# The two pairs of a couple in different PSUM tiles, in the first product by seven block products

## The chip, the core and the metric

The program runs on one core of a Trainium2 chip. The metric is the device time of one execution in microseconds (us); the time before is 593.28 us, the median of three runs (590.06, 593.28 and 599.59 us). One further execution was profiled; the profile shows for each engine when its instructions ran and what ended its idle time: TensorE (PE, with PEld for its weight loads), VectorE (DVE), ScalarE (ACT), GpSimd (POOL), and SyncE (SP), whose queue issues the transfers.

## What is computed

Attention with a narrow window and block summaries, followed by a feed-forward layer with the activation relu(h)². Cut to what matters here:

```python
x = attention(q, k, v)              # (3072, 512)
h = x @ w_in                        # w_in (512, 2048): the first product
g = np.maximum(h, 0.0) ** 2
return g @ w_out                    # w_out (2048, 512): the second product
```

All of it is float32. For TensorE each operand is split into a high and a low float32r part, and a product is the sum of three: high by high, low by high, high by low.

## The kernel before

The 3072 tokens are six units of 512. The first two units go through the feed-forward layer plainly. The other four go in two sets of two units (`s` = 0 and 1). In both sets the second product `g @ w_out` is made by seven block products (a Strassen-like scheme on 2 by 2 blocks, `products`), and in set 1 the first product `x @ w_in` is, too: that is `mixed`, the function that the change touches. It begins when the second product of set 0 ends, and the second product of set 1 follows it to the end of the program.

In `mixed` the 2048 rows of the hidden layer are eight **pairs** `p` = 0 to 7, each of two blocks of 128 rows; the model dimension has two halves, and the 1024 tokens of set 1 are two units. For every pair seven **steps** `j` = 0 to 6 are made, each one block product of six matmuls of 128x512 (`product`, L1647). I write (k, j) for step j of a couple's first pair (k = 0) or second pair (k = 1). Two pairs 2i and 2i+1 make a **couple**, and their steps are interleaved by a table: `COUPLE` is (0,2), (1,2), (0,3), (0,4), (1,3), (1,4), (0,6), (0,5), (1,6), (1,5). The first couple's table `FIRST_COUPLE` also holds steps 0 and 1 of pairs 0 to 3; steps 0 and 1 of pairs 4 to 7 (`BEGINS`) come before everything.

Steps 0, 2, 4 and 6 of a pair add up in one PSUM accumulator `x`, which is read between them: after step 0 (`Q1`), after step 2 (`Q2`), after step 4 (`Q3`) and after step 6 (`Q21`, or `R21` with the relu). So step 4 of a pair has to wait until its own `Q2` has read, and step 6 until its own `Q3` has. Steps 3 and 5 add up in another buffer (`sz`), step 1 in `att`. Pairs 0 to 3 are read by ACT (`evacuate`, L1661, and the relu L1740). Pairs 4 to 7, whose flag `apart` is set, are read by DVE with an addition (`plus`, L1666, which also reads `sz` and `att`); their step 0 lies in another buffer, so `x` begins with step 2. DVE further makes squares (L1674) and differences (L1682), ACT squares by relu and square (L1677, L1678).

The accumulators lie in two PSUM tiles, `o0` and `o1`, each of two halves of 128x512 float32 (2 KB per partition and half): `o_tiles[i // 2][:, i % 2]` for `i` = `slot`, 0 to 3. `Pair.slot` says which half a pair has; pairs p and p+4 have the same one. The same two tiles, whole, are the accumulators of `products` before and after (L1454): its first product in set 1 opens `o0`, its ninth `o1`. `old` names the last readers of the tiles from set 0, `mixed_end` the last readers in `mixed`.

The order of the instructions on every engine is made by a planner (`Plan`): tasks have due times and costs, and a list schedule with buffer counts gives the order, in which they are then emitted. In the planner the four halves are four separate buffers. The semaphore waits between engines are not written in the kernel: the layer below sets them from the tiles that each emitted instruction reads and writes.

Of the kernel before, what the change touches and what calls it, by code (L numbers as in the profile page):

```python
# [240 lines left out]
def attention_then_relu2_ffn(  # L241
# [1340 lines left out]
    def mixed():  # L1582
# [105 lines left out]
        class Pair:  # L1688
            def __init__(self, p):
                self.p, self.apart = p, p >= NQ // 2  # L1690
                self.g = Buf(kinds[f"w{NQ + p}"], (P, 4 * DM), F32, f"g{s}_{p}")
                self.parts = g_parts[s, p] = [Part(self.g, k * DM, (k + 1) * DM) for k in range(4)]
                self.slot = p // 2 % 2 * 2 + p % 2
                self.x = self.bank()

            def bank(self):
# [108 lines left out]
    for u in range(PLAIN + 2):  # L1805
# [14 lines left out]
        if u > PLAIN:  # L1820
            at, rest = unit_at[u], [(j, p) for j in range(SOON, PRODUCTS) for p in range(NQ)]
            rest.insert(NQ + 2, rest.pop(NQ - 1))
            for f in range(NF):
# [5 lines left out]
                for _ in range(WITH_ITEM[f]):  # L1829
                    j, p = rest.pop(0)  # L1830
# [81 lines left out]
```

## Time and profile before

| | |
|---|---|
| median of three runs | 593.28 us (590.06 to 599.59) |
| the profiled execution | 595.69 us, of which its span 592.7 us |
| PE busy | 575.2 us, 97% of the span |
| DVE busy | 443.3 us, 75% |
| ACT busy | 352.9 us, 60% |
| `mixed` after its steps 0 and 1 of pairs 4 to 7 | from 440.8 to 511.7 us |
| second product of set 1 | from 511.7 to 588.3 us |

The profile's views that are used: its page; the busy time of each engine in chosen stretches (engine, busy us, and in brackets the number of instructions; then the granted TensorE clock, the DMA engines' share and GB/s); the waits (who waited for whom: us in total, times, the longest); the chain of work that ended last; and the timeline (start us, duration us, engine, line, operation, what it writes and reads; in square brackets how long the engine was idle before it and what ended that). Buffer numbers are left out in the profile's names, so `o` is `o0` or `o1`, and `g` is a buffer of any pair.

### The profile page before, as it was taken

The page shows a single profiled execution, that of the slowest core. Times are in us where ns is not written, and L with a number is a line of the kernel's source. Part 1 is how long each engine was busy: PE and PEld are TensorE (multiplying, and loading weights), DVE is VectorE, ACT ScalarE, POOL GpSimd, SP SyncE. Part 2 cuts the span into 40 slices and gives each one's busy share as a digit, 9 for nine tenths or more (in the row PEclk, how much of TensorE's full clock was granted, in tenths as well). Part 3 has the DMA queues.
Part 4 walks back from the last instruction along what each step waited for, and adds up shares of the span by engine and source line. Part 5 has one row for each costly group of instructions (what it writes and reads, how often), then busy time and mean ns, then how long its engine had stood idle before and what let it go on. Part 6 is the DMA issues. An engine that isn't in the chain of part 4 may idle for free.

```text
span 592.7 us, 12046 instructions
## 1 busy us (share of the span) xinstructions
PE 575.2 (97%) x4084; PEld 467.6 (79%) x4084; DVE 443.3 (75%) x1018; ACT 352.9 (60%) x876; POOL 98.5 (17%) x165
## 2 busy tenths in 40 slices
PE   8999999999999999999999999999989999999997
PEld 6777878787788888888788888878778877788885
DVE  5899898777547729656976877999839865678764
ACT  1999876767636546645666567586546324654442
POOL 4300005153766014400300050000000000000000
PEclk9999999999999999999999999999989999999999
DMA  8999985869997878995989756898884445667772
GB/s 306 311 391 320 320 295 183 290 225 334 346 336 222 266 277 247 323 305 179 339 243 298 265 181 217 270 295 272 267 264 144 128 146 172 177 191 233 196 225 96
DMA packets 120272, 149.61 MB, mean 252 GB/s; under 512 B 10556, under 2 KB 79164, under 8 KB 120212
## 3 DMA queue, kind: packets, MB, share of 16 engines
q1 hardware_dynamic: 120212, 148.86, 77.1%
q8 instruction: 32, 0.52, 0.3%
q14 instruction: 28, 0.23, 0.1%
HBM read 103.99 MB, written 44.04 MB: 250 GB/s over the span
## 4 chain that ended last, share of the span: by engine, by line
PE 67%; DMA 11%; DVE 10%; ACT 4%; SPq 4%; issue 2%; POOL 2%; DVEq 0%; ACTq 0%
PE o L1454 23%; PE h L1340 14%; PE o L1074 8%; PE o L1647 7%; PE h L1050 6%; DMA raw<-wW 5%; PE sz L1647 3%; PE x L854 3%; DMA kb<-kT 2%; PE att L647 2%; PE att L1647 2%; SPq L841 1%; DMA a<-turn 1%; DVE g L1666 1%; DVE t L995 1%
## 5 line engine op out<-in xcount | busy, mean ns | idle before, releaser
L1454 PE MATMUL o<-gh,w 128*128 128x512 f32 x448 | 121.2, 392 | 0.0
L1436 ACT CAST gh<-g 128x512 fp32r<-128x512 f32 x112 | 68.6, 621 | 56.3 <-PE o L1454 26.5
L1454 PEld LDWEIGHTS o<-gh,w 128*128 128x128 f32 x448 | 83.3, 188 | 17.9 <-ACT gh L1436 0.3
L1441 DVE TENSOR_TENSOR gl<-g,gh 128x512 fp32r<-128x512 f32 x112 | 76.2, 692 | 21.7 <-ACT gh L1436 21.1
L1050 PE MATMUL h<-xh,w 128*128 128x512 f32 x240 | 74.8, 392 | 1.0 <-DVE w L1003 0.7
L1454 PE MATMUL o<-gl,w 128*128 128x512 f32 x224 | 69.5, 391 | 0.4 <-DVE gl L1441 0.3
L1340 PE MATMUL h<-xh,w 128*128 128x512 f32 x224 | 69.0, 389 | 0.0
L1074 PE MATMUL o<-w,gh 128*128 128x512 f32 x240 | 62.2, 395 | 0.4 <-DVE w L1003 0.2
L778 ACT ACTIVATE p<-p,small 128x118 f32<-128x118 f32 x160 | 61.1, 386 | 1.1 <-DVE small L721 0.8
L1050 PEld LDWEIGHTS h<-xh,w 128*128 128x128 f32 x240 | 44.8, 188 | 11.7 <-DVE w L1003 1.3
L1074 PEld LDWEIGHTS o<-w,gh 128*128 128x128 f32 x240 | 44.3, 188 | 10.8 <-ACT gh L1061 0.9
L1454 PEld LDWEIGHTS o<-gl,w 128*128 128x128 f32 x224 | 41.9, 188 | 10.0 <-DVE gl L1441 1.2
L1340 PEld LDWEIGHTS h<-xh,w 128*128 128x128 f32 x224 | 42.1, 188 | 8.7
L1050 PE MATMUL h<-xl,w 128*128 128x512 f32 x120 | 46.7, 389 | 0.0
L1340 PE MATMUL h<-xl,w 128*128 128x512 f32 x112 | 43.6, 389 | 0.0
L1350 ACT ACTIVATE r<-h 128x512 f32<-128x512 f32 x32 | 19.1, 597 | 37.7 <-PE h L1340 37.5
L660 POOL COPY kb<-kb 128x96 f32<-128x96 f32 x25 | 8.5, 339 | 194.7 <-PE att L647 107.3
L1064 DVE TENSOR_TENSOR gl<-r,gh 128x512 fp32r<-128x512 f32 x30 | 23.1, 771 | 19.4 <-ACT gh L1061 16.7
L721 DVE CUSTOM_DVE_ANT_0 p<-att,mask 128x118 f32<-128x118 f32 x152 | 33.1, 275 | 2.6 <-PE att L647 2.5
L1074 PE MATMUL o<-w,gl 128*128 128x512 f32 x120 | 33.6, 390 | 0.0
L1431 DVE TENSOR_TENSOR g<-g 128x512 f32<-128x512 f32 x48 | 32.8, 689 | 0.4
L778 ACT ACTIVATION_READ_ACCUMULATOR p<-p,small 128x1 f32 x160 | 30.5, 190 | 0.0
(209 smaller groups left out, 1079.6 us busy)
## 6 DMA issues: line engine op xcount, KB each, us to landing
raw<-wW SPq DMA_DIRECT2D x32, 512.0 KB
w<-scr_s SPq DMA_DIRECT2D x64, 256.0 KB
w<-scr_a SPq DMA_DIRECT2D x48, 256.0 KB
turn<-a SPq DMA_DIRECT2D x40, 256.0 KB
a<-turn SPq DMA_DIRECT2D x160, 64.0 KB
scr_t<-ci SPq DMA_DIRECT2D x32, 256.0 KB
w<-scr_i SPq DMA_DIRECT2D x32, 256.0 KB
w<-scr_t SPq DMA_DIRECT2D x32, 256.0 KB
```

The costliest lines, as they stand in the source:

```text
L721: nc.vector.tensor_tensor_reduce(out=pr.tile[:, j, :KEYS], in0=score_at(g, 0, j), in1=mask_of(g)[0], scale=-SCALE, scalar=-NEG, op0=ALU.ad ...
L778: nc.scalar.activation(x, score_tile(g, p % parts)[:, p] if by_pe else x, AF.Exp, bias=nm.tile[:, p : p + 1], scale=SCALE if by_pe else -1 ...
L1050: nc.tensor.matmul(cut(h), lhsT=lhs.tile[:, k * P : (k + 1) * P], rhs=rhs[:, k, c0 : c0 + n], start=(i == 0), stop=(i == 3 * KT - 1),)
L1064: lambda: nc.vector.tensor_tensor(out=cut(gl), in0=cut(r), in1=cut(gh).bitcast(F32), op=ALU.subtract),
L1074: nc.tensor.matmul(o_of(o, t), lhsT=terms[i][0].tile[:, (t - t0) * P : (t - t0 + 1) * P], rhs=terms[i][1].tile, start=(first and i == 0), ...
L1340: nc.tensor.matmul(h.tile, lhsT=lhs.tile[:, k * P : (k + 1) * P], rhs=rhs[:, k, c0 : c0 + TU], start=(i == 0), stop=(i == 3 * KT - 1),)
L1350: t2 = add(f"RL{name}", "ACT", 0.56, lambda: nc.scalar.activation(r.tile, h.tile, AF.Relu), due + 2 - R_LEAD, [t1], take=[r], use=[h])
L1431: lambda x=x, ins=ins, op=op: nc.vector.tensor_tensor(out=x.tile, in0=ins[0].tile, in1=ins[1].tile, op=op),
L1436: f"GH{s}_{n}", "ACT", 0.54, lambda x=x, gh=gh: nc.scalar.copy(out=gh.tile, in_=x.tile), due - GH_LEAD, ready,
L1441: lambda x=x, gh=gh, gl=gl: nc.vector.tensor_tensor(out=gl.tile, in0=x.tile, in1=gh.tile.bitcast(F32), op=ALU.subtract),
L1454: nc.tensor.matmul(o.tile[:, d], lhsT=chunk.tile[:, w * HALF + d * P : w * HALF + (d + 1) * P], rhs=y.tile, start=begins and w == 0 and y ...
L1647: nc.tensor.matmul(o.tile, lhsT=lhs(w, k), rhs=y[k], start=begins and i == 0, stop=i == 5, skip_group_check=not begins,)
```

## The change

One expression, the half that a pair's accumulator has:

```diff
             def __init__(self, p):
                 self.p, self.apart = p, p >= NQ // 2
                 self.g = Buf(kinds[f"w{NQ + p}"], (P, 4 * DM), F32, f"g{s}_{p}")
                 self.parts = g_parts[s, p] = [Part(self.g, k * DM, (k + 1) * DM) for k in range(4)]
-                self.slot = p // 2 % 2 * 2 + p % 2
+                self.slot = p % 2 * 2 + p // 2 % 2
                 self.x = self.bank()
```

| pair | 0 | 1 | 2 | 3 | 4 | 5 | 6 | 7 |
|---|---|---|---|---|---|---|---|---|
| before | o0 first | o0 second | o1 first | o1 second | o0 first | o0 second | o1 first | o1 second |
| after | o0 first | o1 first | o0 second | o1 second | o0 first | o1 first | o0 second | o1 second |

Before, a couple's two pairs share a tile, and the next couple has the other tile. After, a couple's first pair has a half of `o0` and its second a half of `o1`; the next couple has the other halves. `old[slot]` and `mixed_end[slot // 2]` go by the slot and follow: pair 1 begins when the last reader of `o1` from set 0 is done, pair 2 when that of `o0` is; and `o0` is given back by pairs 0, 2, 4, 6, `o1` by pairs 1, 3, 5, 7.

The order of the instructions stays the same on all five engines; what differs is the tile they name and what they wait for. In brackets stands the engine (or the DMA queue) whose semaphore an instruction waits for. The first place is DVE, in the couple of pairs 4 and 5 (`g1_4`, `g1_5` are their results): (0,2)'s `Q2`, (1,2)'s `Q2`, then `Q3` of pair 4 and of pair 5, with differences of pair 3 between them.

```order
 L1674 SCALAR_TENSOR_TENSOR g1_3_5417<-g1_3_5417 128x512 [waits DVE_49]
-L1666 TENSOR_TENSOR g1_4_5171<-o0_66,g1_4_5171 128x512 [waits PE_49]
+L1666 TENSOR_TENSOR g1_4_5171<-o0_66,g1_4_5171 128x512 [waits PE_49,Activation_49]
 L1682 TENSOR_TENSOR g1_3_5417<-g1_3_5417 128x512 [waits DVE_49]
-L1666 TENSOR_TENSOR g1_5_5205<-o0_66,g1_5_5205 128x512
+L1666 TENSOR_TENSOR g1_5_5205<-o1_67,g1_5_5205 128x512 [waits PE_49,Activation_49]
 L1682 TENSOR_TENSOR g1_3_5417<-g1_3_5417 128x512 [waits DVE_49]
 L1666 TENSOR_TENSOR g1_4_5171<-o0_66,g1_4_5171 128x512 [waits PE_49]
 L1666 TENSOR_TENSOR g1_4_5171<-sz4_5627,g1_4_5171 128x512 [waits DVE_49]
-L1666 TENSOR_TENSOR g1_5_5205<-o0_66,g1_5_5205 128x512 [waits PE_49]
+L1666 TENSOR_TENSOR g1_5_5205<-o1_67,g1_5_5205 128x512 [waits PE_49]
```

Before, pair 5's first `plus` has no wait for PE of its own: the wait of pair 4's, ahead of it, is already one for the later product, that of pair 5. After, each waits for its own product, and besides for ACT's last read of the same tile.

The second place is PE in the first couple: (0,2) and (1,2), the first products that need the summed operand `xkb`, right behind step 0 of pairs 2 and 3.

```order
-L1647 MATMUL o0_66<-xkb_5349,w7_1035 128x512 [waits Activation_49] x2
-L1647 MATMUL o0_66<-xkb_5349,w7_1035 128x512 x2
+L1647 MATMUL o0_66<-xkb_5349,w7_1035 128x512 [waits Activation_49]
+L1647 MATMUL o0_66<-xkb_5349,w7_1035 128x512 x3
 L1647 MATMUL o0_66<-xa0_5386,w7_1035 128x512 [waits DVE_49]
 L1647 MATMUL o0_66<-xa1_5395,w7_1035 128x512 [waits DVE_49]
-L1647 MATMUL o0_66<-xkb_5349,w7_1035 128x512 [waits DMAHW2_49]
-L1647 MATMUL o0_66<-xkb_5349,w7_1035 128x512 x3
-L1647 MATMUL o0_66<-xa0_5386,w7_1035 128x512
-L1647 MATMUL o0_66<-xa1_5395,w7_1035 128x512
+L1647 MATMUL o1_67<-xkb_5349,w7_1035 128x512 [waits DMAHW2_49,Activation_49]
+L1647 MATMUL o1_67<-xkb_5349,w7_1035 128x512 x3
```

Before, ACT was waited for here only for the operand. After, pair 0's product shares `o0` with pair 2 and pair 1's shares `o1` with pair 3, and each waits for ACT's copy `Q1` of pair 2 or 3 out of the other half.

The third place is PE at the end of `mixed`, where the second product of set 1 (L1454) opens `o0`.

```order
-L1647 MATMUL sz7_5743<-xh_74,w7_1035 128x512 [waits DMAHW2_49]
+L1647 MATMUL sz7_5743<-xh_74,w7_1035 128x512 [waits DMAHW2_49,DVE_49]
 L1647 MATMUL sz7_5743<-xh_74,w7_1035 128x512 x3
 L1647 MATMUL sz7_5743<-xl_75,w7_1035 128x512 x2
-L1454 MATMUL o0_66<-gh1_0_5441,w4_911 128x512 [waits DMAHW3_49]
+L1454 MATMUL o0_66<-gh1_0_5441,w4_911 128x512 [waits DMAHW3_49,DVE_49]
 L1454 MATMUL o0_66<-gh1_0_5441,w4_911 128x512 x3
```

Before, the last reader of `o0` belonged to the couple of pairs 4 and 5. After, it is `Q21` of pair 6, in the last couple, and the opening product waits for DVE.

## The prediction

> **What bounds the kernel now.** I read the page first, then the busy time by stage, the waits inside `mixed`, and the chain behind it.
>
> ```profile
> span 592.7 us, 12046 instructions
> PE 575.2 (97%) x4084; PEld 467.6 (79%) x4084; DVE 443.3 (75%) x1018; ACT 352.9 (60%) x876; POOL 98.5 (17%) x165
> 480.60:496.20 15.60, 14.23 (x62) 11.13 (x61) 9.96 (x16) 4.84 (x9) 0.00 (x0) 1.00 0.50 152
> 496.20:511.75 15.55, 14.18 (x62) 11.10 (x61) 9.03 (x14) 7.09 (x13) 0.00 (x0) 1.00 0.60 170
> 511.75:588.30 76.55, 76.54 (x338) 63.07 (x336) 56.25 (x84) 36.15 (x59) 0.00 (x0) 1.00 0.64 192
> 512.13 76.17 PE o L1454 x336
> ```
>
> TensorE is the bound (97%). Behind `mixed` it runs 336 matmuls in 76.17 us without a gap, 0.2267 us each, so a product of six takes 1.360 us. The whole change lies ahead of that piece, which ends the program: what `mixed` gains, the end gains, as long as the piece stays free of gaps. A couple has ten products and should take 13.60 us; the last two take 15.60 and 15.55, in which PE is idle although DVE is busy for only 9.96 and 9.03 and ACT for 4.84 and 7.09. So nobody's throughput is the limit in these two couples; waits are. From 440 to 512 us they are these:
>
> ```profile
> ACT g L1661 <- PE o L1647: 13.1, 6, 3.5
> DVE g L1666 <- PE o L1647: 11.2, 8, 2.7
> PEld o L1647 <- DVE g L1666: 4.4, 4, 1.2
> DVE g L1682 <- ACT g L1678: 1.0, 2, 0.5
> PEld o L1647 <- ACT g L1740: 0.5, 2, 0.2
> PEld o L1647 <- ACT g L1661: 0.5, 2, 0.2
> ```
>
> PE waits for readers of `o` eight times, four for DVE and four for ACT, while those wait much longer for PE. The timeline of pairs 4 and 5 shows why:
>
> ```profile
> 482.77 0.69 DVE L1674 SCALAR_TENSOR_TENSOR g<-g 128x512 f32<-128x512 f32 x1
> 483.33 1.32 PEld L1647 LDWEIGHTS sz<-xkb,w 128*128 128x128 f32 x6
> 483.75 0.69 DVE L1666 TENSOR_TENSOR g<-o,g 128x512 f32<-128x512 f32 x1 [0.30 <-PE o L1647]
> 484.96 0.68 DVE L1666 TENSOR_TENSOR g<-o,g 128x512 f32<-128x512 f32 x1
> 485.70 0.76 PEld L1647 LDWEIGHTS o<-xr,w 128*128 128x128 f32 x4 [1.05 <-DVE g L1666]
> 486.96 1.33 PEld L1647 LDWEIGHTS sz<-xkb,w 128*128 128x128 f32 x6
> 489.70 0.87 PEld L1647 LDWEIGHTS o<-xw,w 128*128 128x128 f32 x4
> 491.06 0.87 PEld L1647 LDWEIGHTS sz<-xh,w 128*128 128x128 f32 x4
> 491.48 0.69 DVE L1666 TENSOR_TENSOR g<-o,g 128x512 f32<-128x512 f32 x1 [2.67 <-PE o L1647]
> 492.81 0.68 DVE L1666 TENSOR_TENSOR g<-o,g 128x512 f32<-128x512 f32 x1
> 493.55 0.76 PEld L1647 LDWEIGHTS o<-xw,w 128*128 128x128 f32 x4 [1.17 <-DVE g L1666]
> 494.82 0.87 PEld L1647 LDWEIGHTS sz<-xh,w 128*128 128x128 f32 x4
> ```
>
> The `sz` product at 483.33 is (0,3); behind it (0,4) needs only pair 4's `Q2`, the `plus` at 483.75, which ends at 484.44. It starts at 485.70, when the *second* `plus`, pair 5's, has ended (484.96 + 0.68 = 485.64). In the same way pair 5's `Q3` at 491.48 waits 2.67 us, for (0,6), a product of pair 4, begun at 489.70, though its own (1,4) ended earlier; and (1,6) starts at 493.55, when pair 4's `Q21` (492.81 + 0.68 = 493.49) has ended. The two halves of a tile are treated as one: a reader waits for the last product into the tile, and a product for the last reader of it. The Trainium skill, "PSUM — Partial Sum Buffer", section "PSUM bank collisions raise a hardware error", asks that engines be kept apart by bank, and gives a bank as 2 KiB per partition; each half is one, so by that rule the chip needs none of these cross waits. No run here shows an unguarded access, and no number below hangs on it.
>
> **What is removed.** PE runs one product after another, so I measure a stall from the `sz` product's weight load ahead of it to the next one behind it, less two products (2.72 us). For (0,4): 486.96 − 483.33 = 3.63, loss 0.91. For (1,6): 494.82 − 491.06 = 3.76, loss 1.04. Pairs 6 and 7 show the same idle times, so the same losses:
>
> ```profile
> 501.27 0.76 PEld L1647 LDWEIGHTS o<-xr,w 128*128 128x128 f32 x4 [1.05 <-DVE g L1666]
> 509.11 0.76 PEld L1647 LDWEIGHTS o<-xw,w 128*128 128x128 f32 x4 [1.17 <-DVE g L1666]
> ```
>
> That is 2 × (0.91 + 1.04) = 3.90 us, and agrees with the couples' excess over 13.60 (2.00 and 1.95, sum 3.95). In pairs 0 to 3 ACT reads instead, and is nearly in time:
>
> ```profile
> 469.51 1.32 PEld L1647 LDWEIGHTS sz<-xkb,w 128*128 128x128 f32 x6
> 471.06 0.77 PEld L1647 LDWEIGHTS o<-xr,w 128*128 128x128 f32 x4 [0.23 <-ACT g L1661]
> 472.33 1.32 PEld L1647 LDWEIGHTS sz<-xkb,w 128*128 128x128 f32 x6
> 476.41 0.87 PEld L1647 LDWEIGHTS sz<-xh,w 128*128 128x128 f32 x4
> 477.97 0.77 PEld L1647 LDWEIGHTS o<-xw,w 128*128 128x128 f32 x4 [0.24 <-ACT g L1740]
> 479.25 0.87 PEld L1647 LDWEIGHTS sz<-xh,w 128*128 128x128 f32 x4
> ```
>
> Losses: 472.33 − 469.51 − 2.72 = 0.10, and 479.25 − 476.41 − 2.72 = 0.12; the first couple has the same two waits. 2 × 0.22 = 0.44 us. All eight stalls together: 4.34 us.
>
> **What is late next.** Each product still waits for its own pair's reader. A reader can start 1.78 us after its product's first weight load (489.70 to 491.48). (0,4): its product (0,2) is long done when DVE, in its fixed order, is through with L1674 at 482.77 + 0.69 = 483.46; pair 4's `plus` then ends at 484.15. PE would begin at 483.33 + 1.36 = 484.69: 0.54 us to spare. The Trainium skill, the same PSUM page, section "Engine vs sequencer instructions", says that VectorE's queue is strictly first in, first out; by that rule the `plus` cannot pass the L1674 ahead of it, which is the order I used, and the sum is the same with or without it. (1,6) needs pair 5's `Q3`: with (1,4) begun five products into the couple, at 6.80 us, that `plus` can start at 8.58, ends at 9.27, and (1,6) begins at 10.88: 1.61 to spare. The new wait of (0,6) for pair 4's `Q3`, formerly covered by (1,4)'s: (0,4) at 4.08, `plus` from 5.86 to 6.55, (0,6) at 8.16. Nothing else moves in SP's or POOL's order. I cost the rest of the couples at nothing; if the 0.54 were used up, each further microsecond of DVE would cost one again, twice (pairs 4 and 6).
>
> **What is added.** First, in the first couple, (0,2) and (1,2) now wait for ACT's copies of pairs 2 and 3 out of the other half of their tile.
>
> ```profile
> 450.25 0.87 PEld L1647 LDWEIGHTS o<-xh,w 128*128 128x128 f32 x4
> 452.38 1.29 DVE L1549 TENSOR_TENSOR p<-p,xt 128x512 f32<-128x512 f32 x2
> 452.97 0.87 PEld L1647 LDWEIGHTS o<-xkb,w 128*128 128x128 f32 x4
> 453.39 0.59 ACT L1661 COPY g<-o 128x512 f32<-128x512 f32 x1 [2.68 <-PE o L1647]
> 454.33 0.87 PEld L1647 LDWEIGHTS o<-xkb,w 128*128 128x128 f32 x4
> 454.40 0.59 ACT L1661 COPY g<-o 128x512 f32<-128x512 f32 x1
> ```
>
> Before, the first copy ended at 453.98, 1.01 us after (0,2) began, the second at 454.99, 0.66 after (1,2). But the first was idle for 2.68 us, waiting for pair 3's product as well; alone, pair 2's product (450.25) lets it start at 452.03 and end at 452.62, 0.35 ahead of (0,2). The second copy has the cast of `p` ahead of it on ACT, which waits for DVE's first of two subtractions, over by about 452.38 + 0.69 = 453.07; with the 0.50 that ACT took from one instruction to the next (453.39 to 454.40, two instructions) the copy runs from about 453.57 to 454.16, 0.17 ahead of (1,2). I take 0; the bounds are 0 and, if both copies keep their old times, 1.01. Behind a waiting product stands all of PE. A gain is excluded here: both products begin in their turn already.
>
> Second, the opening of the second product waits for DVE's `Q21` of pair 6:
>
> ```profile
> 508.38 0.68 DVE L1666 TENSOR_TENSOR g<-o,g 128x512 f32<-128x512 f32 x1
> 511.74 0.87 PEld L1454 LDWEIGHTS o<-gh,w 128*128 128x128 f32 x4
> ```
>
> It ended at 509.06, 2.68 ahead of the opening. In the changed order it follows (0,6), which begins four products before the end: it can start 5.44 − 1.78 = 3.66 us ahead of the opening and ends 2.97 ahead. Cost 0. Other new waits are for readers three products old or older: 0.
>
> **Sum.** 4.34 − 0 − 0. The profiled execution took 595.69 us (span 592.7 and 2.99 around it): 591.35. It stands 2.41 above the median of the runs, and a new median is what will be compared: 593.28 − 4.34 = 588.94, so 588.9 us.
>
> **The rivals.** *The first couple pays* (chance 0.06). The mechanism is the false wait at the second place, as above; for it speaks the narrow 0.17, against it that ACT's copy was idle for 2.68. It gives 588.9 + 1.0 = 589.9.
>
> *The waits are not the tile's* (0.08): if the two `plus` must both be done for another reason, or if the transfers of weights set the pace of a couple, the stalls stay: 593.3 us. For the second speaks that PE's pace in these couples rises from 10 chunks of 256 KB in 15.6 us to 10 in 13.6 us. Against it: the next stage takes such a chunk every 1.36 us at 192 GB/s, with no gap; and the stalls are put down to DVE. Against the first: each stall ends 0.06 after the other pair's reader.
>
> *DVE's last reader opens late* (0.04): this one is slower. DVE and ACT hand each other the results of a couple (squares, then L1682, 1.0 us of waits so far). If the plus of pair 6 came to stand behind the last couple's ACT work, 7.09 us, instead of beside it, it would end at 509.06 + 7.09 = 516.15 instead of 509.06, and the opening would slip by 516.15 + 0.06 − 511.74 = 4.47; pairs 6 and 7 would gain nothing, pairs 0 to 5 their 2.39. That gives 593.28 + 4.47 − 2.39 = 595.4 us. It decides when the plus ends more than 2.68 + 2.39 = 5.07 us late. Against it: the plus stands ahead of the L1682 that wait for ACT, and DVE works 9.03 us of 15.55.
>
> **How the numbers follow.** The forecast has 0.82. Its own uncertainty is less the sum than the runs: those before reach from 3.2 under their median to 6.3 above. I take 585.5 to 594.5 us: 590.06 − 4.34 = 585.7 is the lowest run with the gain, and the upper end takes in the first two rivals and all but the upper part of the runs; the slower rival, alone, is left out. About 2% (12 us) is what a measurement of this kernel tells from no change, and no case here is that large: faster 0.02, within 0.96, slower 0.02, the two tails for the runs' own scatter.
>
> **What would show it.** Right: no wait of PE for DVE L1666 or ACT L1661 and L1740 inside `mixed`; couples of 13.6 us; the second product of set 1 begins 4.3 us sooner after (0,0) and still runs 76.2 us; DVE's wait for PE at pair 5's `Q3` gone from 2.67 to under 1.5. Wrong: a wait of PE for ACT L1661 at the first `o<-xkb` products (first rival), waits for DVE that remain with the couples at 15.6 (second), or an idle PE at the first L1454 (third).

## The result, and the profile after

The changed kernel takes 590.54 us (median of 20 runs, 588.32 to 594.84), the kernel before, timed beside it, 594.27 us (median of 20 runs, 590.06 to 601.01). The ratio is 0.9931 with a 95% interval of 0.9914 to 0.9949: it is faster by 4.1 us (3.0 to 5.1), which is less than 2%. The profiled execution took 588.60 us.

The page and the chain of the changed kernel:

```profile
span 586.8 us, 12058 instructions
PE 573.3 (98%) x4084; PEld 467.0 (80%) x4084; DVE 443.9 (76%) x1018; ACT 353.0 (60%) x876; POOL 99.2 (17%) x165
506.22 76.17 PE o L1454 x336
```

The last piece is what it was, 76.17 us. The gain lies ahead of it. The busy times by stage, for the last two couples and the second product:

```profile
478.60:492.20 13.60, 13.60 (x61) 11.26 (x60) 9.60 (x16) 5.12 (x10) 0.00 (x0) 1.00 0.59 174
492.20:505.80 13.60, 13.60 (x61) 11.26 (x60) 9.19 (x15) 7.14 (x13) 0.00 (x0) 1.00 0.68 194
505.80:582.40 76.60, 76.58 (x338) 63.06 (x336) 56.24 (x84) 35.92 (x58) 0.00 (x0) 1.00 0.65 193
```

A couple now takes 13.60 us, all of it busy on PE, where it took 15.60 and 15.55. DVE works 9.60 and 9.19 us in them, about what it did (9.96 and 9.03). The waits from 432 to 512 us:

```profile
ACT g L1661 <- PE o L1647: 10.4, 8, 2.1
DVE g L1666 <- PE o L1647: 6.4, 6, 1.4
ACT g L1740 <- PE o L1647: 4.5, 4, 1.5
DVE g L1682 <- ACT g L1678: 0.4, 2, 0.2
PEld x L854 <- DMA a<-turn: 0.5, 1, 0.5
```

All eight waits of PE for a reader of `o` are gone. The readers still wait for PE, but each for its own pair: the longest wait of DVE is 1.4 instead of 2.7 us, that of ACT's copies 2.1 instead of 3.5. The last row is a wait of PE for a transfer of the attention, between (0,0) and (1,0). The length of that piece does not go with the tiles, as the last section shows.

The timeline of pairs 4 and 5, the place of the two long stalls:

```profile
480.32 0.68 DVE L1674 SCALAR_TENSOR_TENSOR g<-g 128x512 f32<-128x512 f32 x1
480.93 0.68 DVE L1666 TENSOR_TENSOR g<-o,g 128x512 f32<-128x512 f32 x1
482.12 0.68 DVE L1666 TENSOR_TENSOR g<-o,g 128x512 f32<-128x512 f32 x1
482.71 0.87 PEld L1647 LDWEIGHTS o<-xr,w 128*128 128x128 f32 x4
487.22 0.69 DVE L1666 TENSOR_TENSOR g<-o,g 128x512 f32<-128x512 f32 x1 [1.30 <-PE o L1647]
489.51 0.87 PEld L1647 LDWEIGHTS o<-xw,w 128*128 128x128 f32 x4
```

(0,4) at 482.71 starts before pair 5's `plus` (482.12 + 0.68 = 482.80) has ended: it waits for pair 4's alone, over at 481.61. Pair 5's `Q3` at 487.22 no longer waits 2.67 us, and (1,6) at 489.51 comes in its turn.

**A measure for the stage.** The two profiled executions differ by 595.69 − 588.60 = 7.09 us, more than the change can be worth. For the change I therefore measure from the first weight load of (1,0), behind the last visit of the attention, to the opening of the second product. Of before, a product of an earlier step, then (0,0), (1,0) and the product behind it, and the busy times of one stretch ahead of them:

```profile
432.49 0.76 PEld L1647 LDWEIGHTS att<-xh,w 128*128 128x128 f32 x4
440.78 0.87 PEld L1647 LDWEIGHTS o<-xh,w 128*128 128x128 f32 x4
443.54 0.76 PEld L1647 LDWEIGHTS o<-xh,w 128*128 128x128 f32 x4
444.81 0.87 PEld L1647 LDWEIGHTS att<-xh,w 128*128 128x128 f32 x4
433.46:436.88 3.42, 3.42 (x9) 2.65 (x9) 2.52 (x3) 0.90 (x2) 0.00 (x0) 0.50 0.94 304
```

Of after, the same product, (0,0), (1,0) and the opening of the second product:

```profile
431.92 0.76 PEld L1647 LDWEIGHTS att<-xh,w 128*128 128x128 f32 x4
438.64 0.87 PEld L1647 LDWEIGHTS o<-xh,w 128*128 128x128 f32 x4
442.00 0.76 PEld L1647 LDWEIGHTS o<-xh,w 128*128 128x128 f32 x4
505.83 0.87 PEld L1454 LDWEIGHTS o<-gh,w 128*128 128x128 f32 x4
```

Before: 511.74 − 443.54 = 68.20 us; after: 505.83 − 442.00 = 63.83 us. The gain is 4.37 us, where 4.34 was forecast. The rest, 7.09 − 4.37 = 2.72 us, is not the change's. Of it 1.19 us lies around the span (2.99 us before, 588.60 − 586.8 = 1.80 after), and 443.54 − 442.00 = 1.54 ahead of (1,0). From the product at 432.49 to (0,0) the execution of before took 8.29 us and that of after 438.64 − 431.92 = 6.72, 1.57 less. That is the clock: before, TensorE was granted only 0.50 of its clock for 3.42 us of it, in which it was busy all the time; after, it had 1.00 there. Another 0.57 us lies ahead of that product, and the piece from (0,0) to (1,0) was 0.60 shorter before than after.

### The profile page after: what moved, and what is told of

It reads as the page before. It is cut to its first block, busy times and chain, and to the rows that moved or that the text cites. A ratio compares the mean times of both kernels' runs of the same rounds, so it can differ in the third digit from the quotient of the medians.

```text
span 586.8 us, 12058 instructions
## 1 busy us (share of the span) xinstructions
PE 573.3 (98%) x4084; PEld 467.0 (80%) x4084; DVE 443.9 (76%) x1018; ACT 353.0 (60%) x876; POOL 99.2 (17%) x165
## 4 chain that ended last, share of the span: by engine, by line
PE 71%; DMA 14%; DVE 5%; SPq 3%; ACT 3%; issue 2%; POOL 2%; DVEq 0%; ACTq 0%
PE o L1454 26%; PE h L1340 15%; PE o L1074 8%; PE o L1647 6%; DMA raw<-wW 6%; PE h L1050 6%; PE sz L1647 4%; PE x L854 3%; PE att L647 2%; DMA qvpa_lent<-vF 2%; DMA turn<-a 2%; DMA a<-turn 1%; PE att L1647 1%; DMA fv_lent<-vS 1%; DMA scr_i<-w 1%
## 5 line engine op out<-in xcount | busy, mean ns | idle before, releaser
L1454 PE MATMUL o<-gh,w 128*128 128x512 f32 x448 | 121.5, 393 | 0.0
L1454 PEld LDWEIGHTS o<-gh,w 128*128 128x128 f32 x448 | 83.1, 188 | 18.4 <-ACT gh L1436 0.8
L1454 PE MATMUL o<-gl,w 128*128 128x512 f32 x224 | 69.5, 391 | 0.0
L1454 PEld LDWEIGHTS o<-gl,w 128*128 128x128 f32 x224 | 41.8, 188 | 9.6 <-DVE gl L1441 0.9
```

Of the source, the lines that this page charges most:

```text
L1454: nc.tensor.matmul(o.tile[:, d], lhsT=chunk.tile[:, w * HALF + d * P : w * HALF + (d + 1) * P], rhs=y.tile, start=begins and w == 0 and y ...
```

## The experiments

My theory: the stalls come from two accumulators that alternate in time sharing a tile, and go with it. The rivals: something else in the change made the gain (which tile is handed over first and last, the first couple, the opening); or DVE's work or the transfers set the pace, and the stalls are only where that shows.

**Pairs 4 to 7 alone.** Against the changed kernel, only the pairs that DVE reads get the new tiles:

```diff
-                self.slot = p % 2 * 2 + p // 2 % 2
+                self.slot = p % 2 * 2 + p // 2 % 2 if self.apart else p // 2 % 2 * 2 + p % 2
```

> Only pairs 4 to 7 (read by DVE) get the new halves; pairs 0 to 3 keep the old ones. Measure: from the first weight load of the second step 0 of the first couple to that of the opening of the last second product, 68.20 us before and 63.83 after. Theory (waits across the halves of one tile, inside a couple): the four waits for DVE go (3.90 us), the four for ACT stay (0.44), so 64.3 us, and about 3.9 us off the time, 0.993 of it. Rival (what counts is which pair takes a tile over from the stage before: here pair 1 still begins in o0): no gain, 68.2 us.

Measured: 590.79 us, ratio 0.9933 (0.9905 to 0.9961) to before at 594.97 us, the median of 29 runs beside this experiment and the next three; stage 64.28 us, so 3.92 of the 4.37 us. The timeline of PE's loads and DVE:

```profile
462.04 0.77 PEld L1647 LDWEIGHTS o<-xr,w 128*128 128x128 f32 x4 [0.23 <-ACT g L1661]
468.95 0.77 PEld L1647 LDWEIGHTS o<-xw,w 128*128 128x128 f32 x4 [0.24 <-ACT g L1740]
482.26 0.69 DVE L1666 TENSOR_TENSOR g<-sz,g 128x512 f32<-128x512 f32 x1 [2.67 <-ACT g L1661]
488.18 0.69 DVE L1666 TENSOR_TENSOR g<-o,g 128x512 f32<-128x512 f32 x1
489.50 0.87 PEld L1647 LDWEIGHTS o<-xr,w 128*128 128x128 f32 x4
```

The four short stalls behind ACT are all there (two are shown, the next couple has the same), the four long ones behind DVE are gone. What 482.26 and 488.18 say is taken up below.

**Pairs 0 to 3 alone.** The converse:

```diff
-                self.slot = p % 2 * 2 + p // 2 % 2
+                self.slot = p // 2 % 2 * 2 + p % 2 if self.apart else p % 2 * 2 + p // 2 % 2
```

> Only pairs 0 to 3 (read by ACT) get the new halves; pairs 4 to 7 keep the old ones. Theory: the four waits for ACT go (0.44 us), the four for DVE stay, 67.76 us on the same measure, and a time within 0.1% of 0.999. Rival (taking over and the first couple's order carry the gain): most of the 4.3 us, about 64 us.

Measured: 594.39 us, ratio 0.9992 (0.9968 to 1.0015); stage 67.83 us, a gain of 0.37. The total can't tell this from nothing; the stage and the rows can.

```profile
487.42 0.76 PEld L1647 LDWEIGHTS o<-xr,w 128*128 128x128 f32 x4 [1.05 <-DVE g L1666]
495.27 0.76 PEld L1647 LDWEIGHTS o<-xw,w 128*128 128x128 f32 x4 [1.17 <-DVE g L1666]
```

The long stalls are there with their old idle times, and the last couple has them again; ACT's are gone. The two parts make 3.92 + 0.37 = 4.29 of 4.37 us: they add up, and neither hides the other.

**The tiles exchanged, the pairs still sharing.** Couples of one tile as before, but the first couple now begins in `o1`, and the last readers of `o0` belong to the last couple, as they do in the changed kernel:

```diff
-                self.slot = p % 2 * 2 + p // 2 % 2
+                self.slot = (1 - p // 2 % 2) * 2 + p % 2
```

> The two pairs of a couple share a tile as before, but the tiles change places: pairs 0, 1, 4, 5 in o1 and 2, 3, 6, 7 in o0. Theory: all eight waits stay, 68.2 us on the same measure, no change in time (ratio 1.000). Rival (it is the handing over of the tiles between the stages that gained): pairs 0 and 1 now begin in the tile that is free earlier, so a gain of up to 4 us. The opening now waits for the last reader of pair 7, which ends 0.24 us ahead of it in the trace of after: cost 0 to 0.1.

Measured: 594.58 us, ratio 0.9992 (0.9967 to 1.0018); stage 68.16 us. All eight stalls are there, of which two:

```profile
457.63 0.76 PEld L1647 LDWEIGHTS o<-xr,w 128*128 128x128 f32 x4 [0.23 <-ACT g L1661]
486.03 0.76 PEld L1647 LDWEIGHTS o<-xr,w 128*128 128x128 f32 x4 [1.05 <-DVE g L1666]
```

Which tile is taken over and given back at which time is worth 0.04 us of the stage. That rival falls.

**The tiles exchanged, the pairs apart.** As the change, with `o0` and `o1` swapped:

```diff
-                self.slot = p % 2 * 2 + p // 2 % 2
+                self.slot = (1 - p % 2) * 2 + p // 2 % 2
```

> As the changed kernel, but the tiles change places: a couple's first pair in o1, its second in o0. The opening of o0 then waits for DVE's last read of pair 7 and no longer for that of pair 6, 2.96 us ahead in the trace of after; pair 7's ended 0.24 ahead. Theory: no wait inside the stage, 63.83 us on the same measure, cost of the opening 0 to 0.1, and the same time as after (0.993 of before). Rival (the opening's wait for DVE decides): PE idle at the opening by 0.3 us or more, 64.1 us or more.

Measured: 590.25 us, ratio 0.9925 (0.9897 to 0.9953); stage 63.81 us, no stall. Here the opening of the second product has to wait for the `Q21` of pair 7 instead of pair 6:

```profile
506.53 0.69 DVE L1666 TENSOR_TENSOR g<-o,g 128x512 f32<-128x512 f32 x1 [0.67 <-PE o L1647]
507.47 0.87 PEld L1454 LDWEIGHTS o<-gh,w 128*128 128x128 f32 x4
```

It ends at 507.22, 0.25 us ahead, and still costs nothing. So the change could have taken either tile for either pair.

**DVE's step made longer, before and after.** If a reader of the other pair holds a product up, more work in both pairs' readers must cost PE twice as much as its own pair's reader would explain. Every `Q2` that DVE makes is issued twice, with the same result; the planner's cost for it, and so the order, stays. (In these kernels the lines behind stand lower: `plus` is L1667.)

```diff
+            def emit():
+                for _ in range(2 if name.startswith("Q2_") else 1):
+                    nc.vector.tensor_tensor(out=to.tile, in0=o.tile, in1=x.tile, op=ALU.add)
...
-                name, "DVE", 0.64, lambda: nc.vector.tensor_tensor(out=to.tile, in0=o.tile, in1=x.tile, op=ALU.add), key, deps,
+                name, "DVE", 0.64, emit, key, deps,
```

In the kernel before:

> The kernel before, with DVE's Q2 of pairs 4 to 7 made twice (the same addition again, the result the same): four more DVE instructions of 0.69 us in the same order. Theory: (0,4) waits for the last reader of the tile, two more additions later, so its stall grows by 1.2 to 1.4 us in each of the two couples: 70.6 to 71.0 us on the measure of the other runs (68.20 before), and a time 2.4 to 2.8 us over before, ratio 1.004 to 1.005. Rival (DVE is not what PE waits for there): unchanged, 68.2 us.

Measured: 600.26 us, ratio 1.0070 (1.0043 to 1.0097) to before at 595.11 us (14 runs beside this experiment and the next); stage 72.18 us, more than the expected 70.6 to 71.0. The timeline of DVE and PE's loads:

```profile
486.37 1.42 DVE L1667 TENSOR_TENSOR g<-o,g 128x512 f32<-128x512 f32 x2 [0.31 <-PE o L1647]
488.31 1.41 DVE L1667 TENSOR_TENSOR g<-o,g 128x512 f32<-128x512 f32 x2
489.77 0.76 PEld L1647 LDWEIGHTS o<-xr,w 128*128 128x128 f32 x4 [2.50 <-DVE g L1667]
506.78 0.76 PEld L1647 LDWEIGHTS o<-xr,w 128*128 128x128 f32 x4 [2.50 <-DVE g L1667]
497.61 0.77 PEld L1647 LDWEIGHTS o<-xw,w 128*128 128x128 f32 x4 [1.17 <-DVE g L1667]
```

PE's idle time at (0,4) grew from 1.05 to 2.50 us in both couples, by 1.45, where I had expected 1.2 to 1.4; that at (1,6), whose `Q21` is not doubled, stayed 1.17. Two single additions with a difference between took 485.64 − 483.75 = 1.89 us before; now it is 489.72 − 486.37 = 3.35, so one extra addition costs 0.73, and (0,4) pays for both, pair 4's and pair 5's. I had worked with about 0.60, the time from one start to the next on different data (483.75 to 484.96 with one instruction between); that the repeated addition has to wait for the first is my reading, which no run separates. That makes 2 × 1.45 = 2.90 of the stage's 72.18 − 68.20 = 3.98. The rest lies ahead of every doubled addition, where the windows of this kernel (of which the granted clock stands third from the end) show what took it:

```profile
439.55:445.07 5.52, 3.48 (x40) 2.64 (x38) 0.69 (x1) 1.86 (x4) 0.00 (x0) 0.90 0.72 194
445.07:447.38 2.31, 2.31 (x8) 1.83 (x7) 1.30 (x3) 1.23 (x3) 0.00 (x0) 0.50 1.01 239
447.38:452.87 5.49, 5.49 (x26) 4.53 (x24) 5.03 (x9) 3.94 (x7) 0.00 (x0) 1.00 0.41 142
```

The piece at 445.07 is (1,0), one product of six, which ran at a granted clock of 0.50 and took 2.31 us, where it took 444.81 − 443.54 = 1.27 in the kernel before, 1.04 more. It followed on a longer wait in the last attention visit in this execution. So this excess is not the additions'; measured instead from (2,0), step 0 of pair 2 further on in the first couple (450.25 before, 452.87 here), the stage is longer by 2.89 us, which is the two stalls.

The total is also above the expected ratio of 1.004 to 1.005, by 5.15 us over before instead of 2.4 to 2.8, though its interval reaches down to 1.0043. The clock bears on this as well. Of the nine runs four have a mean granted clock of 0.999 or more; their median is 597.14 us, that of the eight such runs of before 594.63, a difference of 2.5 us. The other five have 600.32, the other six of before 596.31. These are few runs, divided after the result was known.

In the kernel after:

> The changed kernel with the same four additions made again. Theory: in the trace of after pair 4's Q2 ended 1.10 us ahead of (0,4) and pair 5's 2.6 ahead of (1,4), so one more addition of 0.6 to 0.7 us ahead of the first and two ahead of the second fit: 63.8 us on the same measure, the same time as after (0.993 of before). Rival (DVE now paces the two couples, with no room left): 0.6 to 0.7 us for each couple, 65.1 us or more.

Measured: 589.05 us, ratio 0.9899 (0.9875 to 0.9922); stage 63.85 us, no stall:

```profile
482.63 1.41 DVE L1667 TENSOR_TENSOR g<-o,g 128x512 f32<-128x512 f32 x2
484.42 0.87 PEld L1647 LDWEIGHTS o<-xr,w 128*128 128x128 f32 x4
```

Pair 4's two additions end at 484.04, and (0,4) begins at 484.42 in its turn: the extra 0.72 us are taken out of the margin, 0.38 of which is left. The same extra work costs PE 2.9 us with a shared tile and nothing without. That speaks against DVE's pace as the cause: with four additions more, and DVE busy for 10.88 and 10.47 us, the last two couples still take 13.60 us each:

```profile
480.32:493.92 13.60, 13.60 (x61) 11.26 (x60) 10.88 (x18) 5.12 (x10) 0.00 (x0) 1.00 0.59 175
493.92:507.52 13.60, 13.60 (x61) 11.26 (x60) 10.47 (x17) 7.15 (x13) 0.00 (x0) 1.00 0.70 194
```

The total is 1.9 us lower than the changed kernel's own ratio would give, but the intervals overlap and the stage is the same to 0.02 us, so I take nothing from it.

## Why the prediction was right

**What is removed.** Right in cause and size. The four stalls behind DVE were put at 3.90 us and those behind ACT at 0.44; each part by itself gave 3.92 and 0.37 us, and the whole change 4.37, where 4.34 was forecast. That it is the sharing of the tile is shown from both sides: with the two tiles exchanged the stalls stay if pairs share and go if they don't. One run was not made: the old pairing with each half as a tile of its own. That these are semaphore waits set by the tile, and not something that two neighbouring halves do to each other in the chip, rests on the profile, which names the other pair's reader as what ended each stall, and on the waits listed with the change.

**What is late next.** Nothing, as forecast, but one margin was too small. For pair 4's `Q2` ahead of (0,4) I worked out 0.54 us; it is 482.71 − 481.61 = 1.10. A small part of that, 0.09, is that the `plus` starts 0.61 us after the L1674 ahead of it (480.32 to 480.93), where I had taken 0.69. For the rest, I kept DVE's start as it was before. But DVE waits there for ACT's copies of pair 3, and those too waited for both pairs' products. The kernel with only pairs 4 to 7 changed is the one that my sum described: DVE still waits 2.67 us for ACT at 482.26, the `plus` ends at 488.87, and (0,4) begins at 489.50, 0.63 us later. With pairs 0 to 3 changed as well, ACT gets its copies earlier and hands DVE the other 0.47 us. The error was on the safe side and cost nothing.

**What is added.** Zero, as taken, and the narrow places are as narrow as they were worked out. The first couple of the changed kernel, ACT's copies of pairs 2 and 3 and the products that wait for them:

```profile
450.50 0.59 ACT L1661 COPY g<-o 128x512 f32<-128x512 f32 x1 [1.32 <-PE o L1647]
451.43 0.87 PEld L1647 LDWEIGHTS o<-xkb,w 128*128 128x128 f32 x4
452.09 0.58 ACT L1661 COPY g<-o 128x512 f32<-128x512 f32 x1
452.79 0.87 PEld L1647 LDWEIGHTS o<-xkb,w 128*128 128x128 f32 x4
```

The copies end at 451.09 and 452.67, 0.34 and 0.12 us ahead; the forecast was 0.35 and 0.17. The step that carried it was to see that the copy's old wait of 2.68 us was itself made by the shared tile: it now waits 1.32, for its own product. At the end, pair 6's `Q21` and the opening of the second product:

```profile
502.18 0.69 DVE L1666 TENSOR_TENSOR g<-o,g 128x512 f32<-128x512 f32 x1
```

It ends at 502.87, 2.96 us ahead of 505.83; the forecast was 2.97.

**The signs.** One of the four signs that were named for being right did not come out as worded: counted from (0,0), the second product begins 70.96 − 67.19 = 3.77 us sooner, not 4.3. The piece from (0,0) to (1,0), with the last visit of the attention in it, took 2.76 us before and 3.36 after; I overlooked that it varies by as much as that, and its length does not go with the tiles. The start was moved to (1,0) when the trace of after was known, and before any of the experiments. The other signs hold: no wait of PE for a reader, couples of 13.60 us with 76.17 us behind them, and 1.30 us of wait at pair 5's `Q3`.

**The rivals.** *The first couple pays* falls by the 0.12 us that are left, *the waits are not the tile's* by the exchanged tiles, and its part on transfers by couples of 13.60 us at 174 and 194 GB/s. *DVE's last reader opens late* falls by the 2.96 us.

**The time.** 588.9 us forecast, 590.54 measured. Of the 1.6 us, 0.99 is the level: I set out from 593.28, the median of three runs, and 20 runs gave 594.27. The other 0.6 is the difference of the medians, 3.73 us against a sum of 4.34; the ratio's interval, 3.0 to 5.1 us, holds the sum. The stage, which ran at a granted clock of 1.00 throughout in both traces, gives the sharper number, and it is one execution of each kernel. It came out as 68.16 and 68.20 in the two kernels with all eight stalls at a clock of 1.00, and as 63.81 to 63.85 in the three without any, so that the sum meets it to 0.03 us is no closer than such traces repeat.

## What to carry to other kernels

Where two accumulators take turns, put them in different tiles, even if they are different halves that never overlap: the layer that sets the waits counted the tile here, not the half. Look for it where an engine waits for a reader and that reader waits much longer for the engine, and where the wait ends 0.06 us after an instruction on somebody else's data. And when a false wait goes, work out anew every start that hung on one of its kind: the readers move forward too, which is where the room for the new waits came from.

## What the runs showed of the hardware that was not expected

The piece from (0,0) to (1,0), which holds one product, the last visit of the attention and the waits in it, was 2.76 us long in the kernel before, 3.36 in the kernel after, and up to 5.52 in the others. It does not go with the tiles: with these exchanged it was 4.21 us when the pairs shared a tile and 3.55 when they did not.

In three of the eight profiled executions (there is one of each kernel) TensorE's granted clock fell to 0.50 after a stretch of waits, when PE was just or already busy again: in the kernel before from 433.46 to 436.88, in that with pairs 0 to 3 alone early in the program, from about 27.3 to 30.7, and in the kernel before with the additions made twice. There, by the windows above, it was low for (0.10 × 5.52) / 0.5 = 1.10 us before 445.07 and 2.31 behind it, 3.4 us in all, like the other two. In the first it cost 1.57 us, in the last 1.04 of the stage, both of the order of the effects that were sought here. The Trainium skill, "TensorE: Matmul & The Clock Gate", section "Part 1: The HAM clock gate", gives half the clock after at least one idle window of about 3.4 us, and the full clock again after a busy one. The trace agrees in the half and in the length. PE was not idle throughout the stretch ahead of the fall, though: it was busy for 1.63, 1.26 and 1.41 of the 3.4 us ahead of the three. In the kernel with the tiles exchanged and the pairs apart it was busy for only 1.23 of the 3.4 us from 429.4, and the clock stayed at 1.00. So the busy time alone does not decide it here, and where the limit lies was not tried.
